# Attention scores on quarters of TensorE: 64 queries by 192 keys a product

## The chip, the cores and the metric

One core of a Trainium2 chip runs the whole program, in one launch. The metric is the device time of that launch in microseconds (us), from runs of the same kernel; a profile of one execution goes with them. TensorE multiplies and has two streams in the profile, PE for products and PEld for the loads of their stationary operands. VectorE is DVE, ScalarE is ACT, GpSimd is POOL, SyncE is SP; "PEq", "SPq" and so on are an engine's sequencer.

## The reference

Attention with a sliding window, then a mixture of eight experts, all in float32. Batch 8, 8 heads, 576 positions, 64 numbers a head:

```python
scores = scale * np.matmul(q, k.transpose(0, 1, 3, 2))
rel = pos[:, None] - pos[None, :]
bias = slopes[:, None, None] * (-np.abs(rel))[None]
mask = (rel >= 0) & (rel < 128)
scores = np.where(mask, scores + bias[None], -1e9)
...
attn = exp(scores - max) / sum
x = attn @ v
```

The rows of x (4608 tokens of 512 numbers) go to two of eight experts each, chosen by the two largest noisy logits: relu(x @ w1[e]) @ w2[e], weighted by the softmax of the two logits. A query sees itself and the 127 keys ahead of it, so a block of 64 queries needs 191 keys.

## The kernel before, in words

**Pairs and groups.** The 64 (batch, head) sets are 32 pairs of heads. A pair's queries and keys lie in one tile `qk`, transposed: head 0 on partitions 0 to 63, head 1 on 64 to 127, first the queries (`QW` columns), then the 576 keys. A pair has five blocks of queries, four of 128 and one of 64, in `GROUPS`: blocks 0 and 1, blocks 2 and 3, and the last block, which is taken for two pairs at once. That makes 32 + 32 + 16 = 80 units.

**A unit** (`unit`, line 612) passes from engine to engine. TensorE computes the scores into two banks of PSUM, one a head (`scores`, line 491; `scores_of_last`, line 510). A block of 128 queries is multiplied with the 128 keys of the block before and its own 128 (block 0 with its own alone), so a product is 64 x 128 queries by 128 or 256 keys, and the products of the two heads stand on the two halves of TensorE's rows. For the last blocks, 64 queries of head 0 and 64 of head 1 stand behind each other in columns 512 to 639 of `qk` with zeros on the other head's partitions, and one product over all 128 rows gives both heads' 192 scores; the next bank takes the next pair.

VectorE folds the two halves into one row of 128 keys (`top`, line 518): a masked copy puts a query's own-block keys over the keys that are out of its window, and a custom instruction (line 516) adds the bias and finds the largest. ScalarE takes the exponentials and their sums (`soft`, line 536). TensorE transposes (line 553), ScalarE or VectorE copies out of PSUM (`evac`, lines 267 and 271), GpSimd splits the two key blocks again (lines 573 and 574), TensorE multiplies with the values (`weigh`, line 576; `weigh_last`, line 591).

**After a batch** the rows are normalised and written to memory (`rows`, `row_major`), the gate's logits are made (`gate`, line 759) and the tokens are routed (`route`). The first expert's first 1024 tokens are begun while attention still runs (`first`, products on lines 1272 and 1316); all the other blocks of tokens follow in a second wave, after the last of attention's memory has been given back.

**The order** is made by a planner while the program is built (`Order`, line 97). Each step is given to its engine with a cost and a rank (`pe(us, rank, ...)`), and an engine takes the step of lowest rank that is ready, by the planner's clock. A step that ScalarE or VectorE may do (`either`) goes to whichever takes it first. TensorE's steps have a mode; `like` (line 185) prefers, among steps of nearly the same rank, one of the mode in use, and a change of mode costs `SWITCH`. The scores of full blocks have the mode "rows", the last blocks "full", as the transposes. There are two pairs of banks for scores (`sb`), five tiles `qk` and five of probabilities (`pr`).

**The start.** GpSimd makes number patterns, VectorE the masks from them (`masks`, line 344), and ScalarE or VectorE copies the bias of each head with its slope (`bias_of`, line 360).

Of the kernel before, what the change touches and what calls it, by code (L numbers as in the profile page):

```python
# [22 lines left out]
NP = H // 2  # L23
QW = 512 + 128
GROUPS = ((0, 1), (2, 3), (4,))
# [202 lines left out]
def attention_moe(ctx: ExitStack, tc: tile.TileContext, qk_, v, w_gate, w_noise, noise, w1, w2,  # L228
# [115 lines left out]
    def masks():  # L344
        def window(out_, rel_):

            nc.vector.tensor_scalar(out_, rel_, 0.0, float(W), op0=OP.is_lt, op1=OP.mult)
            nc.vector.tensor_add(out_, out_, rel_)

        def full():  # L350
            nc.vector.tensor_scalar(own_key, rel, 0.0, None, op0=OP.is_ge)
            window(rel2[:, 0], rel)
            nc.vector.tensor_scalar(rel2[:, 1], rel, 0.0, 2.0 ** 40, op0=OP.is_lt, op1=OP.mult)
            nc.vector.tensor_add(rel2[:, 1], rel2[:, 1], rel)

        def halves():
            nc.vector.tensor_scalar(own_key4, rel4[:, 0:64], 0.0, None, op0=OP.is_ge)
            window(relc4, rel4)

        def bias_of(e, h):  # L360
            copy(e, bias[:, :, h], rel2, scale=slope(h))
            part = slice(h % 2 * 64, h % 2 * 64 + 64)
            copy(e, bias4[part, h // 2], relc4[part], scale=slope(h))

        yield dve(0.14, -40, lambda: nc.vector.tensor_scalar(ident, rel, 0.0, None, op0=OP.is_equal))
        yield dve(0.14, -40, lambda: nc.vector.tensor_scalar(before, rel, 0.0, None, op0=OP.is_lt))
        yield dve(1.0, -40, full)
        yield dve(0.6, -40, halves)
        for g in range(NP):
            for h in (2 * g, 2 * g + 1):  # L370
                yield either(0.56, 0.37, -20 + 5 * g, LATE[9], lambda e, h=h: bias_of(e, h))
            mark(biased[g])
# [118 lines left out]
    def scores(k, blocks, s):  # L491
        qk = qks[k]
        for z, i in enumerate(blocks):
            k0, c = (i - 1) * 128 if i else 0, width(i)
            o = place_of(blocks, z)
            for h in range(2):
                half = slice(h * D, h * D + D)
                nc.tensor.matmul(s[h][:, o:o + c], qk[half, i * 128:i * 128 + 128], qk[half, QW + k0:QW + k0 + c],  # L498
                                 start=True, stop=True)

# [9 lines left out]
    def scores_of_last(k, s):  # L510
        for z in range(2):
            qk = qks[k + z]
            nc.tensor.matmul(s[z][:, 0:192], qk[:, 512:QW], qk[:, QW + S - 192:QW + S], start=True, stop=True)

# [15 lines left out]
    def top_of_last(k, s, p, nm):  # L530
        for z in range(2):
            nc.vector.copy_predicated(s[z][:, 0:64], own_key4.bitcast(U32), s[z][:, W:W + 64])
        for z in range(2):
            biased_and_largest(p[:, z, 0], s[z][:, 0:W], bias4[:, (k + z) % NP], nm[:, z, 0:1])

# [7 lines left out]
    def soft_of_last(g, p, nm, den):  # L543
        for z in range(2):
            pv = p[:, z, 0]
            nc.scalar.activation(pv, pv, AF.Exp, bias=nm[:, z, 0:1], scale=-1.0,
                                 accum_out=den[:, 0, 2 * g + 2 * z:2 * g + 2 * z + 1])

# [6 lines left out]
    def evac(e, blocks, t, pt):  # L555

        if blocks == (4,):
            copy(e, pt[:, :, 0], t[:, 0:2 * W].rearrange("p (z c) -> p z c", z=2))
        else:
            copy(e, pt[:, :, 0:2] if blocks[0] == 0 else pt[:, :, 0:4:2], t.rearrange("p (h z c) -> p h z c", h=2, z=2))  # L560

    def split(blocks, pt):

        if blocks == (4,):
            a, b = (pt[:, :, x].rearrange("p z (h c) -> p z h c", h=2) for x in (0, 1))
            pattern = [[0, 2], [0, 2], [1, 64]]
# [24 lines left out]
    def weigh_last(k, pt, o):  # L591

        t = values_[k // 2]
        for z in range(2):
            for at, kb in ((0, 3), (1, 4)):
                for h in range(2):
                    half, hh = slice(h * D, h * D + D), (2 * z + h) * D
                    nc.tensor.matmul(o[half, z * D:z * D + D], t[:, kb, hh:hh + D], pt[:, z, at, half], start=at == 0, stop=at == 1)

# [12 lines left out]
    def unit(u):  # L612
# [5 lines left out]
        if last:  # L618
# [6 lines left out]
        mark(seated)  # L625
        yield pe((0.77, 0.98, 0.53)[gr], r0, lambda: scores_of_last(k, s) if last else scores(k, blocks, s),
                 mode="full" if last else "rows")
        for z in range(k, k + 1 + last):
# [65 lines left out]
    def rows(b, last, t):  # L694
# [6 lines left out]
        def sums():  # L701
            if last:
                nc.vector.tensor_scalar(den[0:64, 0, 1:H:2], den[64:128, 0, 0:H:2], 1e-9, None, op0=OP.add)
                nc.vector.tensor_scalar(den[0:64, 0, 0:H:2], den[0:64, 0, 0:H:2], 1e-9, None, op0=OP.add)
            else:
# [867 lines left out]
    ranks = ranks1 + [1000 + s for s in range(8 * len(second))]  # L1573

    nc.gpsimd.memset(ones, 1.0)
    nc.gpsimd.memset(one, 1.0)
# [4 lines left out]
    nothing = nc.gpsimd.to_reg(0.0)  # L1581
    order.busy["POOL"], order.busy["DVE"], order.busy["ACT"] = 2.5, 1.5, 1.9
    order.at(2.5, lambda: order.dispatch("POOL"))
    order.at(1.5, lambda: order.dispatch("DVE"))
    order.at(1.9, lambda: order.dispatch("ACT"))
# [100 lines left out]
```

## Time and profile before

| | |
|---|---|
| three runs | 1040.87, 1041.65, 1038.19 us; median 1040.87 |
| span of the profiled execution, first to last instruction | 1039.9 us |
| TensorE busy in it | 1006.7 us (97%), 6952 products |
| VectorE busy | 684.7 us (66%) |
| ScalarE busy | 440.4 us (42%) |
| GpSimd busy | 367.3 us (35%) |
| mean granted clock of TensorE | 0.990 |

For the profiled execution the span is the time that the profile gives; the time of that launch as the runs count it is not listed apart. The page of the profile has each engine's busy time; the views behind it show the same execution by stretches of time, by line, by wait and instruction by instruction. A product's record ends when its last result is out, so records overlap and a busy TensorE need not be working at its peak.

### The profile page before, as it was taken

The page shows a single profiled execution, that of the slowest core. Times are in us where ns is not written, and L with a number is a line of the kernel's source. Part 1 is how long each engine was busy: PE and PEld are TensorE (multiplying, and loading weights), DVE is VectorE, ACT ScalarE, POOL GpSimd, SP SyncE. Part 2 cuts the span into 40 slices and gives each one's busy share as a digit, 9 for nine tenths or more (in the row PEclk, how much of TensorE's full clock was granted, in tenths as well). Part 3 has the DMA queues.
Part 4 walks back from the last instruction along what each step waited for, and adds up shares of the span by engine and source line. Part 5 has one row for each costly group of instructions (what it writes and reads, how often), then busy time and mean ns, then how long its engine had stood idle before and what let it go on. Part 6 is the DMA issues. An engine that isn't in the chain of part 4 may idle for free. (4 is left out here: it accounts for less than half of the span.)

```text
span 1039.9 us, 20426 instructions
## 1 busy us (share of the span) xinstructions
PE 1006.7 (97%) x6952; PEld 613.2 (59%) x6952; DVE 684.7 (66%) x2410; ACT 440.4 (42%) x1218; POOL 367.3 (35%) x572
## 2 busy tenths in 40 slices
PE   8998999989999999999999999999999999999996
PEld 6776766656557645654574457456644754584454
DVE  8988999997756857744777566467636834773311
ACT  8976887762222524332342344134313421442211
POOL 4356686664633203331232233143203320332202
PEclk9999999989999999999999999999999999999998
DMA  9856989835399879893997489859957794864223
GB/s 345 297 173 209 310 306 307 291 72 142 59 251 188 203 200 177 134 207 107 182 205 173 73 175 187 203 78 171 208 156 106 152 189 153 172 132 68 37 24 49
DMA packets 193338, 178.61 MB, mean 172 GB/s; under 512 B 104080, under 2 KB 147376, under 8 KB 193232
## 3 DMA queue, kind: packets, MB, share of 16 engines
q1 hardware_dynamic: 175888, 138.35, 49.2%
q0 software_dynamic: 17344, 38.94, 23.9%
q8 instruction: 55, 0.90, 0.4%
q14 instruction: 51, 0.42, 0.1%
HBM read 117.29 MB, written 40.71 MB: 152 GB/s over the span
## 5 line engine op out<-in xcount | busy, mean ns | idle before, releaser
L1405 POOL DMA_INDIRECT out_dram<-yo,ix x69 | 110.4, 1600 | 497.5 <-ACT yo L267 448.3
L1292 ACT ACTIVATE hh<-bank 128x384 f16<-128x384 f32 (+9 forms) x192 | 92.9, 484 | 449.4 <-PE bank L1272 442.5
L1307 DVE SCALAR_TENSOR_TENSOR hl<-bank,hh 128x384 f16<-128x384 f32 (+9 forms) x200 | 108.8, 545 | 255.9 <-ACT hh L1292 255.0
L1316 PEld LDWEIGHTS <-hh 128*128 128x128 f16 (+1 forms) x944 | 92.2, 98 | 100.2
L1272 PE MATMUL bank<-xh,w1hb 128*128 128x512 f16 (+8 forms) x384 | 127.0, 331 | 0.4 <-DMA xh<-th 0.4
L1272 PE MATMUL bank<-xh,w1lb 128*128 128x512 f16 (+8 forms) x384 | 127.1, 331 | 0.0
L1272 PE MATMUL bank<-xl,w1hb 128*128 128x512 f16 (+8 forms) x384 | 126.9, 330 | 0.1
L1272 PEld LDWEIGHTS <-w1ha 128*128 128x128 f16 x832 | 80.5, 98 | 48.8
L1272 PEld LDWEIGHTS <-w1hb 128*128 128x128 f16 x768 | 75.3, 98 | 55.5 <-issue 2.3
L1272 PE MATMUL bank<-xh,w1ha 128*128 128x384 f16 (+8 forms) x320 | 102.0, 319 | 0.0
L1272 PE MATMUL bank<-xh,w1la 128*128 128x384 f16 (+8 forms) x320 | 102.0, 319 | 0.0
L1272 PE MATMUL bank<-xl,w1ha 128*128 128x384 f16 (+8 forms) x320 | 102.0, 319 | 0.0
L540 ACT ACTIVATE p<-p,nm 128x128 f32<-128x128 f32 x256 | 99.0, 392 | 5.6 <-DVE nm L516 5.6
L1316 PE MATMUL bank<-w2ha,hl 128*128 128x512 f16 x244 | 92.5, 379 | 0.3 <-DVE hl L1307 0.3
L1316 PE MATMUL bank<-w2ha,hh 128*128 128x512 f16 x244 | 92.5, 379 | 0.0
L1316 PE MATMUL bank<-w2la,hh 128*128 128x512 f16 x244 | 92.5, 379 | 0.0
L1316 PE MATMUL bank<-w2hb,hl 128*128 128x512 f16 x228 | 86.4, 379 | 0.7 <-DVE hl L1307 0.7
L1316 PE MATMUL bank<-w2hb,hh 128*128 128x512 f16 x228 | 86.4, 379 | 0.0
L1316 PE MATMUL bank<-w2lb,hh 128*128 128x512 f16 x228 | 86.4, 379 | 0.0
L1219 POOL DMA_INDIRECT xg<-xs_dram,ix x69 | 73.8, 1070 | 32.4 <-issue 14.8
L1316 PEld LDWEIGHTS <-hl 128*128 128x128 f16 x472 | 46.4, 98 | 57.5 <-DVE hl L1307 2.4
L498 PE MATMUL bank<-qk 64*128 64x256 f32 (+1 forms) x512 | 67.1, 385 | 7.0 <-DMA qk<-in_qk_dram 4.6
(250 smaller groups left out, 2036.3 us busy)
## 6 DMA issues: line engine op xcount, KB each, us to landing
raw<-in_w_dram SPq DMA_DIRECT2D x144, 256.0 KB, 4.8
mraw<-in_w_dram SPq DMA_DIRECT2D x56, 512.0 KB, 4.1
qk<-in_qk_dram SPq DMA_DIRECT2D x32, 608.0 KB, 5.3
vraw<-in_v_dram SPq DMA_DIRECT2D x16, 640.0 KB, 6.6
out_dram<-xg SPq DMA_DIRECT2D x10, 1024.0 KB, 7.6
xs_dram<-x SPq DMA_DIRECT2D x32, 256.0 KB, 5.4
xg<-xs_dram,ix POOLq DMA_INDIRECT x69, 5.8
xh<-th SPq DMA_TRANSPOSE x69, 6.0
```

Of the source, the lines that this page charges most:

```text
L498: nc.tensor.matmul(s[h][:, o:o + c], qk[half, i * 128:i * 128 + 128], qk[half, QW + k0:QW + k0 + c], start=True, stop=True)
L540: nc.scalar.activation(pv, pv, AF.Exp, bias=nm[:, z, h:h + 1], scale=-1.0, accum_out=den[:, i, 2 * g + h:2 * g + h + 1])
L1219: yield pool(1.04, rank, lambda: nc.gpsimd.indirect_dma_start(out=xg[0:r], out_offset=None, in_=xs[0:blk.rows], in_offset=bass.IndirectOff ...
L1272: nc.tensor.matmul(t[:, 0:blk.n], wp[:, c], x[:, c, 0:blk.n], start=c == 0 and z == 0, stop=c == 3 and z == 2)
L1292: nc.scalar.activation(o, i, AF.Relu)
L1307: yield dve(0.07 + c * 0.00104, rank - MIDDLE, lambda: nc.vector.scalar_tensor_tensor(hl[:, 0:c], t[:, 0:c], 0.0, hh[:, 0:c], op0=OP.max, ...
L1316: nc.tensor.matmul(blk.y[j][0:r], h[:, cs], wp, start=f == 0 and m == 0, stop=f == 7 and m == 2)
L1405: ins = nc.gpsimd.indirect_dma_start(out=out, out_offset=bass.IndirectOffsetOnAxis(ap=blk.ix[0:r, j:j + 1], axis=0), in_=t[0:r], in_offset ...
```

## The change

Every product of scores becomes one of 64 queries by 192 keys (128 for block 0) on a quarter of TensorE: the head chooses the half of the rows, the half block of queries the half of the columns. Of the 256 scores of a query, the 64 that lie outside its window anyway are no longer computed. The last blocks of two pairs become four such products, and a bank of PSUM now holds one head of both pairs, where it held both heads of one pair; the bias tile, the sums and the product with the values follow. The queries are loaded without the columns of zeros. A quarter of each bank is no longer written by the products; four fills at the start set the banks to zero. The planner's costs and modes are changed for these steps, and its VectorE begins at 2.5 us in place of 1.5.

```diff
-QW = 512 + 128
+QW = S
...
-            part = slice(h % 2 * 64, h % 2 * 64 + 64)
-            copy(e, bias4[part, h // 2], relc4[part], scale=slope(h))
+            part = slice(h // 2 % 2 * 64, h // 2 % 2 * 64 + 64)
+            copy(e, bias4[part, h // 4 * 2 + h % 2], relc4[part], scale=slope(h))
...
-            for h in range(2):
-                half = slice(h * D, h * D + D)
-                nc.tensor.matmul(s[h][:, o:o + c], qk[half, i * 128:i * 128 + 128], qk[half, QW + k0:QW + k0 + c],
-                                 start=True, stop=True)
+            for a in (0, 64):
+                first_, c_ = (a, c - 64) if i else (0, c)
+                for h in range(2):
+                    half = slice(h * D, h * D + D)
+                    nc.tensor.matmul(s[h][a:a + 64, o + first_:o + first_ + c_], qk[half, i * 128 + a:i * 128 + a + 64],
+                                     qk[half, QW + k0 + first_:QW + k0 + first_ + c_], start=True, stop=True)
...
-            nc.tensor.matmul(s[z][:, 0:192], qk[:, 512:QW], qk[:, QW + S - 192:QW + S], start=True, stop=True)
+            for h in range(2):
+                half = slice(h * D, h * D + D)
+                nc.tensor.matmul(s[h][z * 64:z * 64 + 64, 0:192], qk[half, 512:QW], qk[half, QW + S - 192:QW + S],
+                                 start=True, stop=True)
...
-                    nc.tensor.matmul(o[half, z * D:z * D + D], t[:, kb, hh:hh + D], pt[:, z, at, half], start=at == 0, stop=at == 1)
+                    nc.tensor.matmul(o[half, z * D:z * D + D], t[:, kb, hh:hh + D], pt[:, h, at, z * D:z * D + D], start=at == 0, stop=at == 1)
...
-        yield pe((0.77, 0.98, 0.53)[gr], r0, lambda: scores_of_last(k, s) if last else scores(k, blocks, s),
-                 mode="full" if last else "rows")
+        yield pe((0.66, 0.77, 0.43)[gr], r0, lambda: scores_of_last(k, s) if last else scores(k, blocks, s),
+                 mode="quads")
...
-                nc.vector.tensor_scalar(den[0:64, 0, 1:H:2], den[64:128, 0, 0:H:2], 1e-9, None, op0=OP.add)
-                nc.vector.tensor_scalar(den[0:64, 0, 0:H:2], den[0:64, 0, 0:H:2], 1e-9, None, op0=OP.add)
+                lower, upper = (den[z:z + 64, 0].rearrange("p (a b) -> p a b", b=4) for z in (0, 64))
+                nc.vector.tensor_scalar(lower[:, :, 2:4], upper[:, :, 0:2], 1e-9, None, op0=OP.add)
+                nc.vector.tensor_scalar(lower[:, :, 0:2], lower[:, :, 0:2], 1e-9, None, op0=OP.add)
...
+    for t in bank[0:4]:
+        nc.vector.memset(t, 0.0)
...
-    order.busy["POOL"], order.busy["DVE"], order.busy["ACT"] = 2.5, 1.5, 1.9
+    order.busy["POOL"], order.busy["DVE"], order.busy["ACT"] = 2.5, 2.5, 1.9
...
-    order.at(1.5, lambda: order.dispatch("DVE"))
+    order.at(2.5, lambda: order.dispatch("DVE"))
...
-    qk[..., 0:512], qk[..., QW:] = q[..., 0:512], k
-    for h in range(2):
-        qk[:, h, :, 512 + 64 * h:512 + 64 * h + 64] = q[:, h, :, 512:]
+    qk[..., 0:QW], qk[..., QW:] = q, k
```

What is left out here does the same exchange of pair and head in the largest values, the exponentials, the copy and the split of the last blocks (`top_of_last`, `soft_of_last`, `evac`, `split`), with the same number of instructions.

## Rows read from the trace of the kernel before

**Rows 1.** The page, busy time of each engine.
```profile
PE 1006.7 (97%) x6952; PEld 613.2 (59%) x6952; DVE 684.7 (66%) x2410; ACT 440.4 (42%) x1218; POOL 367.3 (35%) x572
```
**Rows 2.** Windows by stage: from:to, length, busy (records), clock, DMA share, GB/s.
```profile
13.00:100.00 87.00, 84.19 (x872) 61.19 (x873) 79.21 (x439) 71.35 (x307) 46.61 (x101) 1.00 0.74 249
20.00:60.00 40.00, 40.00 (x414) 30.11 (x414) 38.35 (x207) 38.05 (x169) 15.81 (x33) 1.00 0.86 291
100.00:220.00 120.00, 109.31 (x1151) 79.83 (x1151) 115.26 (x591) 93.64 (x368) 82.47 (x164) 0.97 0.87 283
220.00:262.00 42.00, 42.00 (x362) 27.77 (x359) 35.54 (x145) 18.43 (x62) 22.09 (x42) 0.96 0.39 100
328.00:1039.90 711.90, 697.25 (x4105) 400.20 (x4103) 402.42 (x1037) 227.53 (x405) 185.39 (x205) 0.99 0.72 145
```
**Rows 3.** Timeline of TensorE, 213 to 233: start, length, records, [idle before, releaser].
```profile
213.06 0.55 PE L875 MATMUL bank<-hot,hot 128*80 128x64 f16 x10 [3.01 <-DVE gw L1235]
...
231.14 0.33 PE L1272 MATMUL bank<-xhe,w1ha 128*128 128x384 f16 x1
```
**Rows 4.** Waits (total, times, longest): VectorE 13:100, then 100:220, then TensorE.
```profile
DVE xu L271 <- PE bank L589: 2.2, 2, 1.4
DVE lt L775 <- PE bank L770: 1.6, 2, 1.0
...
DVE x L737 <- PE bank L734: 1.1, 2, 0.8
DVE bank L524 <- PE bank L498: 0.6, 2, 0.4
...
PE bank L498 <- DMA qk<-in_qk_dram: 4.6, 1, 4.6
```
**Rows 5.** Timeline of TensorE, 59.6 to 70.6, runs of records of one line.
```profile
61.17 0.69 PE L598 MATMUL bank<-pT,vraw 128*64 128x64 f32 x16
...
62.81 1.13 PE L498 MATMUL bank<-qk 64*128 64x256 f32 x8
63.87 0.66 PE L553 MATMUL bank<-ident,p 128*128 128x128 f32 x4
64.46 1.06 PE L759 MATMUL bank<-xu,wgn 128*32 128x512 f32 x8
...
66.13 0.82 PE L513 MATMUL bank<-qk 128*128 128x192 f32 x4
...
69.57 0.93 PE L498 MATMUL bank<-qk 64*128 64x128 f32 x8
```
**Rows 6.** Records of lines 498 (69.5:70.4) and 598 (61.1:61.7): ns min/median/max, starts.
```profile
L498 PE MATMUL bank<-qk x8: 272/374/378, 69.6 to 70.1; 64*128 64x128 f32 x4, 64*128 64x256 f32 x4
...
L598 PEld LDWEIGHTS bank<-pT,vraw x16: 132/138/138, 61.2 to 61.6; 128*64 128x64 f32 x16
```
**Rows 7.** Timeline of all engines, 0 to 16.
```profile
1.45 0.24 DVE L365 TENSOR_SCALAR ident<-raw 128x128 f32<-128x128 f32 x1 [1.45 <-POOL raw L1577]
...
3.62 4.10 ACT L267 ACTIVATE bias<-raw 64x128 f32<-64x128 f32 x13 [0.15 <-DVE raw L348]
...
3.98 0.52 POOL L413 MEMSET xg<- 128x512 f32 x1
...
6.24 0.50 DVE L524 COPY_PREDICATED bank<-own_key,bank 128x128 f32<-128x128 uint32 x2 [2.65 <-PE bank L498]
...
11.05 0.69 DVE L271 COPY pT<-bank 128x512 f32<-128x512 f32 x1
```
**Rows 8.** Windows of line 498 alone: PE and PEld busy (records), clock, DMA.
```profile
13.00:100.00 87.00, 28.16 (x224) 18.14 (x224) 1.00 0.74 249
100.00:220.00 120.00, 29.32 (x235) 18.84 (x237) 0.97 0.87 283
```
**Rows 9.** Lines of VectorE, 13 to 100: busy us, mean ns, idle before.
```profile
L1177 DVE TENSOR_REDUCE wam<-raw 128x1 f32<-128x512 f32 x8 | 5.4, 672 | 0.0
```
**Rows 10.** A window behind a long wait of TensorE, columns as in rows 2.
```profile
213.40:216.90 3.50, 3.39 (x25) 2.15 (x23) 3.36 (x12) 0.78 (x2) 2.91 (x6) 0.51 1.09 258
```

More of the change, by code (lines that the diff above doesn't have):

```diff
@@ L530, in top_of_last @@
     def top_of_last(k, s, p, nm):
[L531 to L534, printed above, removed]
+        for h in range(2):
+            nc.vector.copy_predicated(s[h][:, 0:64], own_key4.bitcast(U32), s[h][:, W:W + 64])
+        for h in range(2):
+            biased_and_largest(p[:, h, 0], s[h][:, 0:W], bias4[:, k % NP + h], nm[:, h, 0:1])
     def soft(g, blocks, p, nm, den):
@@ L543, in soft_of_last @@
     def soft_of_last(g, p, nm, den):
[L544 to L547, printed above, removed]
+        for h in range(2):
+            pv = p[:, h, 0]
+            nc.scalar.activation(pv, pv, AF.Exp, bias=nm[:, h, 0:1], scale=-1.0,
+                                 accum_out=den[:, 0, 2 * g + h:2 * g + h + 1])
     def trans(p, t, nh):
@@ L557, in evac @@
         if blocks == (4,):
-            copy(e, pt[:, :, 0], t[:, 0:2 * W].rearrange("p (z c) -> p z c", z=2))
+            copy(e, pt[:, :, 0], t[:, 0:2 * W].rearrange("p (h c) -> p h c", h=2))
         else:
@@ L564, in split @@
         if blocks == (4,):
-            a, b = (pt[:, :, x].rearrange("p z (h c) -> p z h c", h=2) for x in (0, 1))
+            a, b = (pt[:, :, x].rearrange("p h (z c) -> p h z c", z=2) for x in (0, 1))
             pattern = [[0, 2], [0, 2], [1, 64]]
```

## The prediction

> **What bounds the kernel now.** I read the page first. TensorE is busy 97% of the span, no other engine over 66% [rows 1]. So I cut the span into stages [rows 2]. From 328 us on, the second wave of expert products holds TensorE for 697 of 712 us; the change touches nothing there. Scores (lines 498 and 513) lie ahead of that, before 262 us. From 13 to 100 us TensorE is busy 84.2 of 87 us and waits only 2.8 in all; VectorE has 79.2, ScalarE 71.4. From 100 to 220 it is VectorE that is full, 115.3 of 120, and TensorE lacks 10.7. From 220 to 262 TensorE is full again, because at 231 the first expert products arrive and fill every hole [rows 3]. The view of waits says the same from the other side [rows 4]: in the first stretch VectorE waits for TensorE (2.2 + 1.6 = 3.8 us lead its list), and in the second TensorE waits for VectorE (3.0 us at once before 213 [rows 3]), while VectorE's own waits for TensorE have shrunk to 1.1 + 0.6 = 1.7.
>
> Past 220 us the end is the sum of TensorE's remaining work: whatever has been done earlier by then comes off the end. So the question is how much of the saved TensorE time turns into earlier work, and how much into waiting.
>
> **What one unit of scores costs.** Three units are shown, from the first record's start to the last one's end [rows 5]: 0.93 us for blocks 0 and 1, 1.13 for blocks 2 and 3, 0.82 for the last blocks. Each float32 product is two records (32 pairs make 64 such units of eight records, 512). A record of 128 columns lasts 272 ns, one of 256 lasts 378: 0.83 ns a column, or 53 ns for 64 columns [rows 6]. The products of two heads lie side by side: blocks 2 and 3 make four steps of 256 columns, 4 x 0.213 = 0.85; blocks 0 and 1 two steps of 128 and two of 256, 0.64. Both leave 0.28 or 0.29 us. The last unit, in the shape of the transposes ahead of it, is four steps of 192 columns one after another, 4 x 0.16 = 0.64, and leaves 0.18, the tail of a last record. So going into a shape costs about 0.1; going out the same, since the line behind the second unit starts 1.06 after it began (62.81 to 63.87), 0.21 over its steps.
>
> **What the change takes off.** (1) Blocks 1 to 3 stream 192 columns instead of 256 in each step, if four quarters run side by side. Four steps in a unit of blocks 2 and 3 save 4 x 0.053 = 0.213; 32 units, 6.8 us. In blocks 0 and 1 only block 1 gets shorter: 0.107 x 32 = 3.4. Block 0 still streams 128.
> (2) A last unit becomes two steps instead of four: 0.32 x 16 = 5.1 us. It leaves the transposes' shape for its own, so it may pay up to two more changes, or none beside another unit of scores: 0 to 3.2 us. I take one each, 1.6, since the planner prefers like beside like; 3.5 stays.
> That is 13.7 us of TensorE time. Four abreast with quarters in both directions is not in this trace. The nearest rows: the gate's products, four strips of 32 output rows, are eight records of 512 columns in 1.06 us; at 0.43 for a step, one after another would be 3.4, so four do run abreast. And line 598 sends sixteen records of 64 columns, weights as narrow as the new ones, in 0.69 us with the last one's tail, a pair in some 0.06 [rows 5]: short loads keep up. The records double (512 to 1024, 64 to 128), which these rows say costs nothing. Bounds of (1) and (2): from 13.7 saved to none, and the rivals below go beyond.
>
> Those loads of line 598 start while products of the same 128 rows are in flight: sixteen loads of 138 ns, their starts within some 0.4 us [rows 6]. By these rows the saving is 13.7 us. A rule speaks against it: the Trainium skill (TensorE: Matmul & The Clock Gate, Part 3: Packing small matmuls — row/col tiling) says that a weight load overlaps running products only where the row group differs, and two of the four quarters of a step share theirs. By that rule it would be about nothing, the third rival; the trace does not bear the rule out for column strips.
>
> (3) The four fills on VectorE at the start, 128x512 in PSUM. Nearest rows: GpSimd's fill of that size 0.52 us, VectorE's copy of that size 0.69, so 2.1 to 2.8 us in all [rows 7]. VectorE's first work is at 1.45, when the first number pattern is there, and it idles 2.65 us before its first score work at 6.24. Fills begun by 0.8 end between 2.9 and 3.6 and push the masks back by 1.5 to 2.1, which that idle time hides. On ScalarE it does not hide: its bias copies, 3.62 to 7.72, wait for the masks (0.15 us before them), and its exponentials come behind them. Bounds 0 and 2.1 us, less what the planner hands to VectorE; I take 1.4. Against it stands what the first scores save, below. If the cover were gone (VectorE busy up to 6.24) the whole 2.1 would show.
> (4) The loads of queries and keys shrink by a twentieth (1216 to 1152 columns). TensorE waits on them only at the start, 4.6 us [rows 4], and 1/19 of that is at most 0.3. I take none: elsewhere they are hidden behind four loads in reserve.
> (5) VectorE's and ScalarE's work on the last blocks, now by head instead of by pair, has the same number and size of instructions, the sums of line 703 too: 0, even uncovered. The exchange of pairs and heads in the transposed copy and line 598 is addressing: 0.
> (6) The planner gets other costs and a new shape, so the order moves on every queue. No row prices that. What one ill-placed step can cost now is the 3.0 us that TensorE waits at its longest [rows 3]. Bounds -3 and +3; I take 0.
>
> **What of it reaches the end.** Of the 512 records of line 498, 224 lie between 13 and 100 us and 235 between 100 and 220 [rows 8]; I spread the last units alike. The first stretch then saves 13.7 x 224/512 = 6.0 us. VectorE must follow, and what it waits for TensorE there now is 3.8, so 3.8 counts. The second saves 6.3, of which by the same reason 1.7 counts; 4.6 becomes new waiting. The other 53 records are 1.4 us, half of it after 220, where it counts, half in the start: 0.7 - 1.4 = -0.7. Sum 3.8 + 1.7 + 0.7 - 0.7 = 5.5 us. The span shown is 1039.9, and the median of the runs 1040.9, 1.0 more, with runs from 1038.2 to 1041.7; against the median that makes 1035.4. Less than 0.3% (3.1 us) could not be told from no change.
>
> **The rivals.** First, VectorE takes it all: it is full already from 20 to 60 us (38.4 of 40) and from 100 to 220 [rows 2], so a faster TensorE only waits. For it: the busy shares. Against it: part of that can slide to where VectorE is freer, as the eight reductions of weights (5.4 us, line 1177) before 100 [rows 9]. It leaves the 0.7 after 220 less the start: 1040 to 1041, no change. The Trainium skill (TensorEngine Tiling (Array Packing), PSUM Bottleneck) has this as its warning, that tiling speeds up products and not the emptying of PSUM; this trace agrees from 100 to 220 and not before.
> Second, the clock. It falls to its lower level, 1.2 GHz, at times: granted 0.51 from 213.4 to 216.9, just after TensorE had waited 3.0 us for VectorE [rows 3, 10], and the stages' means of 0.97 and 0.96 [rows 2] put it at an estimated 7.2 and 3.4 us in all. A stretch like that one loses up to 1.7 us of TensorE. With 4.6 us more of waiting there could be more of them; four, 6.8 us, would eat the gain: 1041.
> Third, weights not hidden: each step of quarters shows its 64-column load, 0.06. Four steps give 0.24: blocks 2 and 3 lose their 0.213, blocks 0 and 1 grow by 0.13 (4.2 us in all), last units keep 0.2 of 0.32 (3.2, less 1.6 of changes). Net +3.5 of TensorE, about two thirds of it felt: 1043.
> Fourth, slower: the change does not do what it says, and the quarters of one head run one after the other, two abreast in place of four. Its place is every unit. Blocks 2 and 3: eight steps of 0.16 against 0.85, +0.43; blocks 0 and 1 likewise +0.43; the last units stay. 64 x 0.43 = 27 us more, all of the 44% before 100 felt, of the 46% after it little more than the 10.7 of waiting does not hold: 12 + 2 + 1, with 1.6 of changes and the start some 18: 1059. It decides once a step of four takes over 0.21.
>
> **How the numbers follow.** The forecast has 0.64 (1027 to 1038: all 13.7 saved, or half of my sum). VectorE's rival 0.16, the clock 0.07, weights 0.06, two abreast 0.07. Faster is 0.63 of the first, 0.03 of the second and 0.02 of the clock: 0.68. Slower is two abreast, 0.07, half of the weights, 0.03, and 0.02 each of the clock and of the second, where a worse order comes on top: 0.14. The rest, 0.18, is the same. The range, 1027 to 1043, leaves out mostly the fourth and the ends.
>
> **What would show it.** Right: four records of 192 columns starting within some 20 ns, a step each 0.16 us; units of 0.82 and 0.92 us, and 0.5 to 0.6 for the last; TensorE's waits from 100 to 220 grown by 4 to 5 us, VectorE's idle time from 13 to 100 (7.8) down by about 4; the first expert product some 5 us before 231. Wrong: steps of 0.21 or more; a first exponential more than 1.4 us later; more stretches at 0.5 of the clock; a first expert product no earlier than 231 with less attention left behind it would move the gain to another place, and with as much behind it would end it.

## The result, and the profile after

The changed kernel takes 1046.89 us (median of 7 runs, 1042.83 to 1050.25) against 1040.41 (7 runs, 1037.52 to 1041.88) for the kernel before on the same chip: a ratio of 1.0055, 95% interval 1.003 to 1.0081. By the medians it is 6.5 us slower; the forecast was 5.5 us faster, 1035.4, with 1043 as the upper end of its range. The span of the profiled execution is 1045.1 us, 5.2 more than before.

The page of the changed kernel, busy time by engine [rows 1]: 576 products more, TensorE's busy time 6.6 us less, VectorE's and GpSimd's 2.9 and 4.0 more.

```profile
PE 1000.1 (96%) x7528; PEld 597.5 (57%) x7528; DVE 687.6 (66%) x2410; ACT 440.6 (42%) x1222; POOL 371.3 (36%) x572
```

The products of scores do what was forecast. The timeline of TensorE in the changed kernel, 59 to 72 us (start, length, records) [rows 5]:

```profile
59.99 0.78 PE L500 MATMUL bank<-qk 64*64 64x128 f32 x16
...
61.28 0.88 PE L500 MATMUL bank<-qk 64*64 64x192 f32 x16
62.10 1.07 PE L765 MATMUL bank<-xu,wgn 128*32 128x512 f32 x8
...
66.54 0.56 PE L517 MATMUL bank<-qk 64*64 64x192 f32 x8
```

A unit of blocks 2 and 3 lasts 0.88 us (1.13 before), one of blocks 0 and 1 0.78 (0.93), a last one 0.56 (0.82). Windows of the scores' lines alone, 0 to 262 us (from:to, length, PE busy, PEld busy, clock, DMA share, GB/s), give the sum. The kernel before, lines 498 and 513:

```profile
0.00:262.00 262.00, 67.09 (x512) 43.38 (x512) 0.98 0.75 244
...
0.00:262.00 262.00, 13.56 (x64) 10.01 (x64) 0.98 0.75 244
```

and the changed kernel, lines 500 and 517:

```profile
0.00:262.00 262.00, 57.29 (x1024) 35.27 (x1024) 0.99 0.74 241
...
0.00:262.00 262.00, 9.62 (x128) 3.99 (x128) 0.99 0.74 241
```

80.65 us became 66.91: 13.7 us saved on these lines, the sum of terms (1) and (2). Not all of it is TensorE's gain: the 288 records of transposes in the same window take 48.1 us where they took 45.2. Windows of line 553 in the kernel before and of line 558 in the changed one:

```profile
0.00:262.00 262.00, 45.22 (x288) 31.82 (x288) 0.98 0.75 244
```
```profile
0.00:262.00 262.00, 48.11 (x288) 31.63 (x288) 0.99 0.74 241
```

**Where it went.** I cut the span at two marks that mean the same work in every version: the first product of the first wave of experts (it reads `xhe`) and the first of the second wave (it reads `xh`). Windows of the kernel before (columns as in [rows 2]):

```profile
0.00:231.10 231.10, 212.81 (x2165) 154.83 (x2166) 213.55 (x1136) 184.95 (x753) 140.76 (x303) 0.98 0.79 260
...
231.10:328.60 97.50, 97.20 (x688) 58.50 (x687) 68.93 (x240) 28.32 (x61) 41.11 (x64) 1.00 0.72 155
```

Windows of the changed kernel, the last two rows being the stretches whose idle time the prediction gave numbers for:

```profile
0.00:223.30 223.30, 201.59 (x2737) 139.13 (x2737) 210.03 (x1125) 182.23 (x745) 141.11 (x301) 0.98 0.79 262
...
223.30:333.50 110.20, 100.76 (x689) 58.40 (x686) 75.75 (x252) 31.19 (x74) 43.61 (x67) 0.97 0.64 145
333.50:1045.10 711.60, 697.71 (x4108) 400.02 (x4106) 401.86 (x1034) 227.17 (x404) 186.55 (x205) 1.00 0.71 145
...
13.00:100.00 87.00, 86.42 (x1220) 60.49 (x1212) 82.05 (x461) 81.95 (x354) 52.72 (x115) 1.00 0.76 257
...
100.00:220.00 120.00, 103.74 (x1397) 72.06 (x1393) 114.30 (x586) 87.73 (x344) 82.55 (x157) 0.97 0.83 268
```

Up to the first mark the changed kernel is 7.8 us ahead. The second wave takes 711.6 us, as before (711.3). All of the loss is between: 110.2 us for 97.5, with the same number of products (689 and 688), so no attention was left behind. Of these 12.7 us, 9.1 are waiting (110.20 - 100.76 = 9.44, against 0.30), and 3.6 are products that ran longer, at a mean granted clock of 0.97 for 1.00 (an estimated 0.03 x 110.2 = 3.3). In the sum: -7.8 + 12.7 + 0.3 = 5.2.

The waits of the changed kernel in that stretch, 262 to 345 us (total, times, longest; columns as in [rows 4]):

```profile
PE bank L1322 <- DVE hl L1313: 6.8, 2, 4.6
...
DVE fit L1246 <- DMA xg<-xs_dram,ix: 5.9, 2, 4.5
```

The same two rows in the kernel before:

```profile
DVE fit L1240 <- DMA xg<-xs_dram,ix: 3.3, 3, 2.3
...
PE bank L1316 <- DVE hl L1307: 0.3, 1, 0.3
```

The longer of TensorE's two waits, 4.6 us, is half of all its waiting there. The timelines of GpSimd, VectorE and TensorE in the changed kernel show how it comes about:

```profile
303.17 0.96 POOL L1225 DMA_INDIRECT xg<-xs_dram,ix  x1 [13.69 <-DVE ix L1023]
304.44 0.95 POOL L1225 DMA_INDIRECT xg<-xs_dram,ix  x1 [0.30 <-issue]
305.69 0.95 POOL L1225 DMA_INDIRECT xg<-xs_dram,ix  x1 [0.30 <-issue]
...
306.94 1.61 POOL L1411 DMA_INDIRECT out_dram<-yo,ids  x1 [0.22 <-issue]
...
308.85 1.56 POOL L1411 DMA_INDIRECT out_dram<-yo,ids  x1 [0.27 <-issue]
...
310.72 1.55 POOL L1411 DMA_INDIRECT out_dram<-yo,ids  x1 [0.26 <-issue]
312.58 1.50 POOL L1225 DMA_INDIRECT xg<-xs_dram,ix  x1 [0.30 <-issue]
...
324.09 0.69 DVE L1246 TENSOR_REDUCE fit<-xg 128x1 f32<-128x512 f32 x1 [4.53 <-DMA xg<-xs_dram,ix]
...
326.48 0.75 DVE L1313 SCALAR_TENSOR_TENSOR hl<-bank,hh 128x256 f16<-128x256 f32 x2
...
326.95 0.61 PE L1322 MATMUL bank<-w2ha,hl 128*128 128x512 f16 x1 [4.64 <-DVE hl L1313]
```

The fourth gather of a block of tokens for the second wave stands on GpSimd behind three scatters of results of the first wave. VectorE comes to the step that needs it (line 1246) and stands there 4.53 us, until 324.09, 11.5 us after the gather was issued; the halves `hl` that TensorE needs for the first wave's second products are queued behind that step and come at 326.48. TensorE waits 4.64 us, and after that it runs at the lower level (1.2 GHz) for a while, as a window of the same kernel shows:

```profile
326.90:329.90 3.00, 2.95 (x8) 1.04 (x9) 2.25 (x12) 0.72 (x1) 0.00 (x0) 0.51 0.52 104
```

In the kernel before GpSimd issues the four gathers in a row, before the first of the scatters (308.67):

```profile
298.63 1.23 POOL L1219 DMA_INDIRECT xg<-xs_dram,ix  x1 [8.61 <-DVE ix L1017]
300.17 0.94 POOL L1219 DMA_INDIRECT xg<-xs_dram,ix  x1 [0.31 <-issue]
301.42 0.95 POOL L1219 DMA_INDIRECT xg<-xs_dram,ix  x1 [0.30 <-issue]
302.67 0.95 POOL L1219 DMA_INDIRECT xg<-xs_dram,ix  x1 [0.30 <-issue]
```

The other long wait, 2.2 us (2.17, at 284.56), stands in the same way behind a gather of the first wave (`xg<-xs_dram,cl`), for which VectorE waits 3.3 us.

So the theory after the profile: the products gain what was forecast, and the order that the planner makes from its new numbers loses more than that where the two waves meet.

### The profile page after: what moved, and what is told of

The parts are those of the page before. It is cut to its first block, busy times and chain, and to the rows that moved or that the text cites. A ratio compares the mean times of both kernels' runs of the same rounds, so it can differ in the third digit from the quotient of the medians.

```text
span 1045.1 us, 21578 instructions
## 1 busy us (share of the span) xinstructions
PE 1000.1 (96%) x7528; PEld 597.5 (57%) x7528; DVE 687.6 (66%) x2410; ACT 440.6 (42%) x1222; POOL 371.3 (36%) x572
## 5 line engine op out<-in xcount | busy, mean ns | idle before, releaser
L1298 ACT ACTIVATE hh<-bank 128x384 f16<-128x384 f32 (+9 forms) x188 | 90.8, 483 | 434.5 <-PE bank L1278 413.5
L1322 PEld LDWEIGHTS <-hh 128*128 128x128 f16 (+1 forms) x944 | 92.2, 98 | 100.1 <-issue 1.4
L1225 POOL DMA_INDIRECT xg<-xs_dram,ix x69 | 75.9, 1100 | 39.8 <-DVE ix L1023 19.5
L1322 PEld LDWEIGHTS <-hl 128*128 128x128 f16 x472 | 46.5, 99 | 66.0 <-DVE hl L1313 10.7
L267 ACT ACTIVATE th<-xg,fit 128x512 f16<-128x512 f32 (+5 forms) x76 | 54.3, 718 | 49.6 <-DVE fit L1238 38.3
```

The source lines that it names most:

```text
L267: nc.scalar.activation(o, i, AF.Copy, **kw)
L1225: yield pool(1.04, rank, lambda: nc.gpsimd.indirect_dma_start(out=xg[0:r], out_offset=None, in_=xs[0:blk.rows], in_offset=bass.IndirectOff ...
L1298: nc.scalar.activation(o, i, AF.Relu)
L1322: nc.tensor.matmul(blk.y[j][0:r], h[:, cs], wp, start=f == 0 and m == 0, stop=f == 7 and m == 2)
```

## The experiments

Each ratio is to the kernel before on the same chip. "Profiled" is the time of the one execution that the profile shows; the last three columns are its stages: to the first mark, between the marks, the second wave.

| run | median us | ratio [95%] | profiled us | to first | between | second |
|---|---|---|---|---|---|---|
| before | 1040.41 | 1 | not listed | 231.1 | 97.5 | 711.3 |
| after | 1046.89 | 1.0055 [1.003, 1.0081] | 1046.89 | 223.3 | 110.2 | 711.6 |
| e1_old_order | 1038.48 | 0.9974 [0.9958, 0.999] | 1037.14 | 226.2 | 98.2 | 711.0 |
| e2_new_order | 1052.35 | 1.0097 [1.0064, 1.0131] | 1052.08 | 230.7 | 103.8 | 715.8 |
| e3_new_costs_only | 1043.38 | 1.002 [1.0003, 1.0038] | 1043.08 | 223.9 | 105.2 | 712.3 |
| e4_new_mode_only | 1040.81 | 0.9992 [0.9974, 1.0009] | 1039.8 | 225.9 | 100.1 | 712.1 |
| e5_no_fills | 1034.35 | 0.9931 [0.9909, 0.9953] | 1034.13 | 226.1 | 96.9 | 709.4 |
| e6_vector_load | 1038.62 | 0.9971 [0.9952, 0.999] | 1035.39 | 227.3 | 97.0 | 709.4 |
| e7_gather_later | 1048.73 | 1.0063 [1.0039, 1.0087] | 1050.45 | 223.0 | 101.0 | 724.7 |
| e8_nudged | 1045.5 | 1.0049 [1.0027, 1.0071] | 1050.66 | 232.7 | 99.0 | 717.2 |
| e9_junction | 1043.29 | 1.0002 [0.9984, 1.002] | 1043.19 | 224.4 | 103.7 | 713.3 |
| e10_no_fills_new_order | 1047.4 | 1.0028 [1.0008, 1.0049] | 1051.18 | 224.4 | 113.3 | 711.8 |
| e11_fills_only | 1043.08 | 1.0002 [0.9992, 1.0013] | 1043.1 | 231.7 | 98.4 | 711.2 |
| e12_junction_no_fills | 1041.74 | 1.0 [0.9984, 1.0017] | 1043.63 | 226.4 | 102.3 | 713.2 |
| e13_old_order_again | 1037.28 | 0.9977 [0.9957, 0.9997] | 1034.04 | 226.2 | 97.0 | 709.1 |
| e14_no_fills_again | 1033.91 | 0.9944 [0.9924, 0.9964] | 1034.53 | 226.0 | 96.9 | 709.9 |
| e15_scalar_load | 1037.09 | 0.9972 [0.9954, 0.999] | 1037.82 | 226.8 | 97.4 | 711.9 |
| e16_gpsimd_load | 1032.9 | 0.9938 [0.9915, 0.9961] | 1032.76 | 224.4 | 96.9 | 709.7 |

How far a single execution can be trusted shows where one kernel was profiled twice. e1 and e13 agree at the first mark (226.2 and 226.2) and part behind it, by 1.2 us between the marks and 1.9 in the second wave; e5 and e14 part by 0.1, nothing and 0.5. So behind the first mark a stage that differs by some 2 us says little. And some profiled executions lie far from their medians: e8's is the slowest of its five runs, 5 us above the median, e10's is 4 us above, e13's 3 us below.

**Products and order apart.** e1 is the changed kernel with the planner's numbers of before, so that every engine's sequence is that of before, apart from the fills (in the traces the two agree instruction by instruction):

```diff
-        yield pe((0.66, 0.77, 0.43)[gr], r0, lambda: scores_of_last(k, s) if last else scores(k, blocks, s),
-                 mode="quads")
+        yield pe((0.77, 0.98, 0.53)[gr], r0, lambda: scores_of_last(k, s) if last else scores(k, blocks, s),
+                 mode="full" if last else "rows")
...
-    order.busy["POOL"], order.busy["DVE"], order.busy["ACT"] = 2.5, 2.5, 1.9
+    order.busy["POOL"], order.busy["DVE"], order.busy["ACT"] = 2.5, 1.5, 1.9
...
-    order.at(2.5, lambda: order.dispatch("DVE"))
+    order.at(1.5, lambda: order.dispatch("DVE"))
```

e2 is the reverse: the products of before, with the planner's numbers of the change; its sequences are those of the changed kernel.

> All of the change's products, fills and loads, but the planner's old costs, modes and start, so every engine works off the same order as before the change. Theory A (the quarters do what they should, the loss is the new order's): faster than before by 4 to 9 us, 1031 to 1037, since the record-level saving of some 13 us is then set against an order that fits the transfers; the wait of 4.6 us behind VectorE near 327 us is gone. Theory B (VectorE and ScalarE bound the attention, and what TensorE saves only comes back as waiting): 1038 to 1042. Theory C (something in the quarters or the fills costs more than the records show): 1043 to 1048, as with the change.

> The products, loads and start of before, but the planner's new costs, mode and start, so the order of the change. Theory A: slower than the change, 1048 to 1060, because the new order's waits stay and TensorE has 10 to 14 us more to do. Theory B: 1043 to 1049, as the change, since TensorE's own work then does not matter. Theory C: 1038 to 1042, as before.

e1 is 2.8 us faster than the kernel before, e2 some 10 us slower (0.0097 x 1041). The order is worth +0.97% with the old products (e2) and about +0.8% with the new (after against e1); the products with their fills -0.26% in the old order (e1) and about -0.4% in the new (after against e2; the comparisons of after with e1 and with e2 are between sets of runs). By its time e1 misses its first theory (1031 to 1037) and lies where the second was put (1038 to 1042: what TensorE saves comes back as waiting). e2, at 1052.4, came in the range of the first theory alone. So the order costs what the change was to gain and more, and in the old order a good part of the saving does come back as waiting. Windows of e1:

```profile
0.00:226.20 226.20, 201.87 (x2742) 140.81 (x2743) 212.49 (x1138) 183.99 (x752) 141.11 (x303) 0.98 0.80 261
...
226.20:324.40 98.20, 97.63 (x689) 58.41 (x687) 68.77 (x241) 28.48 (x64) 41.18 (x65) 1.00 0.76 154
```

In the old order the middle stage has no hole (98.2 us) and the first mark is 4.9 us earlier than in the kernel before. In the new order the old products lose 6.3 us there too, and 4.5 in the second wave. Windows of e2:

```profile
230.70:334.50 103.80, 98.88 (x689) 58.28 (x686) 75.56 (x250) 30.85 (x72) 42.94 (x66) 0.98 0.65 154
334.50:1050.30 715.80, 698.12 (x4108) 400.10 (x4106) 401.37 (x1034) 227.23 (x404) 186.32 (x205) 1.00 0.70 144
```

**Which number moved it.** e3 takes the new costs alone, e4 the new mode alone; e8 is the kernel before with one cost raised by a hundredth:

```diff
-        yield pe((0.77, 0.98, 0.53)[gr], r0, lambda: scores_of_last(k, s) if last else scores(k, blocks, s),
+        yield pe((0.78, 0.98, 0.53)[gr], r0, lambda: scores_of_last(k, s) if last else scores(k, blocks, s),
```

> The change with the planner's new costs, but its old modes and VectorE's old start. Another order again. Theory A: the time depends on how the order happens to meet the transfers, anything from 1032 to 1050, and goes with TensorE's waits between 220 and 345 us, not with the records of the scores, which stay as in the change. Theories B and C: 1043 to 1048, like the change.

> The change with the planner's new mode (all scores alike), but its old costs and VectorE's old start. Theory A: as for the run before, 1032 to 1050 by TensorE's waits between 220 and 345 us. Theories B and C: 1043 to 1048.

> The kernel before, with one cost of the planner changed by a hundredth of a microsecond (0.77 to 0.78 for the scores of blocks 0 and 1) and nothing else. It reorders as many instructions as the change does. Theory A (an order that has not been fitted to the transfers loses several microseconds, whatever made it): 1043 to 1052. Rival (the new costs and the new mode make a worse order of their own): 1039 to 1043.

Neither number alone gives the whole loss: the costs put 7.0 us into the middle stage (105.2 against e1's 98.2), the mode 1.9, which is hardly more than two executions of one kernel differ by. VectorE's later start, the third number, was not tried alone. The time of e3 (1043.4) fits all its theories, that of e4 (1040.8) the first alone. And e8, whose products are those of before, is 0.49% slower by nothing but another order, as its first theory had it; in its profiled execution, the slowest of five, the second wave shows it most (717.2 us for 711.3). So another order can cost as much as the gain that was sought. That the kernel before has an order that suits it better than most I infer from this run and from e2, e3 and e4; one nudge is no survey of orders.

**The place.** e7 and e9 are the changed kernel, with a longer time in the planner for the gathers of the second wave, all of them in e7, those of its first three blocks in e9:

```diff
-        yield max(order.now + 3.4, order.transfer(order.now, 2048.0 * r))
+        yield max(order.now + (8.0 if blk in second[:3] else 3.4), order.transfer(order.now, 2048.0 * r))
```

> The change, with one number of the planner altered: it counts 8 us instead of 3.4 from the issue of a gather of the second wave to its rows, so VectorE's scaling of those rows stands later in its queue. The order of attention stays. Theory A (the loss is VectorE standing in its queue at a gather that has not landed, with the products' halves behind it): TensorE's waits between 262 and 345 us fall from 7 us to under 3, the first product of the second wave comes at 326 to 329 us instead of 333, and the time is 1038 to 1043. Rival (the loss lies elsewhere): 1045 to 1049.

> The change, with the planner's 8 us in place of 3.4 for the gathers of the first three blocks of the second wave alone: attention and the second wave from its fourth block on keep the change's order. (With all blocks altered the second wave began at 324 us and not at 333, but lost 13 us later on, where its order had changed as well.) Theory A (the change loses its time between the first product of the first wave, at 223 us, and that of the second, at 333, where TensorE waits behind VectorE at a gather): the second wave begins at 324 to 329 us and the end follows, 1036 to 1042. Rival (what is gained there is always lost again later): 1044 to 1049.

Both shorten the middle stage, to 101.0 and 103.7 us from 110.2. e7 pays for it behind (724.7 us), and its time is the rival's. e9 keeps most, and with it the change stands level with the kernel before: 1.0002 against 1.0055, with intervals that do not meet; its time, 1043.3, lies between what the theory (1036 to 1042) and the rival (1044 to 1049) gave. So over half a per cent of the loss hangs on the order around the meeting of the waves. Windows of e9:

```profile
224.40:328.10 103.70, 98.43 (x682) 58.18 (x679) 69.56 (x228) 28.80 (x68) 42.58 (x66) 0.97 0.58 146
```

The hole did not close: 5.3 us of waiting are left, and the clock is still at 0.97. But it is another wait. GpSimd still issues the fourth gather behind three scatters (315.65), yet VectorE no longer stands at it, and TensorE's wait of 4.64 us is gone. What is left at its longest stands behind the gather of the first wave, which the edit did not touch. The timelines of VectorE and TensorE in e9:

```profile
284.82 0.69 DVE L1246 TENSOR_REDUCE fit<-xg 128x1 f32<-128x512 f32 x1 [4.45 <-DMA xg<-xs_dram,cl]
...
286.02 0.61 PE L1322 MATMUL bank<-w2ha,hl 128*128 128x512 f16 x1 [3.31 <-DVE hl L1313]
```

That wait was 2.2 us in the changed kernel. No run gave this gather more time too, and none moved the fourth gather ahead of the scatters.

**The fills.** Here the first unit of full blocks in each pair of banks streams all 256 keys, which writes every quarter of the banks once and makes the fills needless (the added scores are masked like the others outside the window): e5 and e14 on e1, e10 on the changed kernel, e12 on e9. e11 is the kernel before with the four fills, and e13 is e1 once more, beside e14 on one chip.

```diff
+            whole = (id(s), blocks[0]) not in written
+            written.add((id(s), blocks[0]))
...
-                first_, c_ = (a, c - 64) if i else (0, c)
+                first_, c_ = (a, c - 64) if i and not whole else (0, c)
...
-    for t in bank[0:4]:
-        nc.vector.memset(t, 0.0)
```

> The run with the old order, without the four fills; the first unit of full blocks in each pair of banks streams all 256 keys instead, so that nothing unwritten is read. Theory A with the fills on the path (the first exponentials come 1.4 us later than before the change, and VectorE and ScalarE are full until 60 us, so the delay goes through): 1.0 to 1.5 us faster than the run with the old order, about 1037.3. Rival (the delay is used up in the holes between 60 and 100 us): no difference, 1038.2 to 1038.8.

> The change and its order, without the four fills; the first unit of full blocks in each pair of banks streams 256 keys. If the fills cost what they did in the old order (4 us): 1042 to 1044. If they are worth only the 1.4 us that the first exponentials come later: 1045 to 1046. If the order decides what becomes of a start that is earlier: anything up to 1048.

> The kernel before with the four fills on VectorE ahead of its masks and nothing else. If the fills delay the first exponentials by 1.4 us and the full engines pass that on: slower than before by 1 to 4 us, ratio 1.001 to 1.004. If TensorE, which binds before 100 us with the old products, makes up for it: within 0.5 us, ratio 0.9995 to 1.0005.

> The run with the later gathers of three blocks, and without the fills. Theory A: the sum of both, 1033 to 1040, near the run with the old order and no fills (1034.4) or better. Rival: 1042 to 1047.

> The change's products in the order of before, fills kept, as in the run of that kernel above, here beside the same kernel without the fills on one chip. If the fills cost something (theory): 0.995 to 0.999 of the kernel before, and 2 to 5 us behind the kernel without them. If they cost nothing (rival): within 1.5 us of it.

> The change's products in the order of before, without fills. If the fills cost something: 0.991 to 0.995 of the kernel before, first expert product near 226 us. If not: the two intervals cover each other, both near 0.995.

In the old order the kernel without fills is the faster one twice: 0.9931 against e1's 0.9974, and on one chip 0.9944 against 0.9977, where the intervals just overlap, by 0.0007. e13 and e14 came where their theory had them; e5, at 1034.4, gained more than its own (1.0 to 1.5 us). The other pairs show 0.0027 (after and e10, overlapping) and 0.0002 (e9 and e12), and fills added to the old products (e11) cost nothing that can be told, as its rival said. e12, expected at 1033 to 1040 as the sum of two gains, came at 1041.7. The profiled executions of e13 and e14 differ by 0.2 us at the first mark and by 0.5 at the end, the other way; but that of e13 is one of its three fastest of twelve. So the price lies between nothing (e11, e12) and 0.43%, some 4.5 us (e5 against e1). In the old order it does not lie before the first mark, where the four executions with and without fills differ by 0.2 us at most; no row shows its place behind it. e10, at 1047.4, fits only the loosest of its forecasts (anything up to 1048): it has the wait of the changed kernel again, longer, with 113.3 us between the marks. TensorE's waits in it, 225 to 345 us:

```profile
PE bank L1326 <- DVE hl L1317: 9.9, 3, 6.2
```

Without fills in the old order the change is faster than the kernel before, by 0.56% (e14) and 0.69% (e5).

**Who sets the pace before the first mark.** Spare work on one engine in each of the 80 units, into a tile that nothing reads: on VectorE in e6 (on e1), on ScalarE in e15 and on GpSimd in e16 (both on e14).

```diff
+        nc.vector.memset(dummy, 0.0)
```
```diff
+        nc.scalar.activation(dummy, ident[:, 0:64], AF.Exp)
```
```diff
+        nc.gpsimd.memset(dummy, 0.0)
```

> The run with the old order, with one more small fill of a spare tile on VectorE in each of the 80 units of scores, some 0.1 us each, 8 to 10 us in all. If VectorE binds attention now and takes up what TensorE saves: slower than the run with the old order by 5 to 9 us, 1043 to 1047. If its full look is work that can slide: by 0 to 3 us, 1038 to 1041.

> The kernel without fills, with one more exponential of 64 columns into a spare tile on ScalarE at the head of each of the 80 units: an estimated 0.3 us each, 64 of them (19 us) ahead of the first expert product. If ScalarE's step of each unit sets TensorE's pace before the first wave (theory): that product 5 us or more later than near 226, the time 5 to 15 us above the run without load. If nothing on ScalarE binds (rival): under 1.5 us later, time within 2 us.

> The kernel without fills, with a fill of a spare tile of 128x64 on GpSimd at the head of each of the 80 units' splits: an estimated 0.1 to 0.3 us each, 6 to 19 us ahead of the first expert product. If GpSimd's split sets TensorE's pace (theory): that product 3 us or more later than near 226, the time 3 to 10 us above the run without load. If not (rival): under 1.5 us later, time within 2 us.

The groups of the spare work, one of e6 (64 of its 80), two of e15, one of e16 (busy us, mean ns, idle before):

```profile
L526 DVE MEMSET dummy<- 128x64 f32 x64 | 7.2, 112 | 0.1
```
```profile
L547 ACT ACTIVATE dummy<-ident 128x64 f32<-128x64 f32 x64 | 16.5, 258 | 0.0
L555 ACT ACTIVATE dummy<-ident 128x64 f32<-128x64 f32 x16 | 4.1, 258 | 0.0
```
```profile
L574 POOL MEMSET dummy<- 128x64 f32 x80 | 13.6, 170 | 0.2
```

These are 9.0 us of records on VectorE, 20.6 on ScalarE and 13.6 on GpSimd. But the records overlap those beside them, and the engines' busy time up to the first mark grew by less: on VectorE by 2.9 us (212.5 in e1, above, to 215.4), on ScalarE by 9.9 (184.1 in e14 to 194.1), on GpSimd by 6.8 (141.3 to 148.1). Windows of e6, then of e14, e15 and e16:

```profile
0.00:227.30 227.30, 201.84 (x2741) 140.07 (x2742) 215.38 (x1218) 184.55 (x752) 141.19 (x303) 0.98 0.80 260
```
```profile
0.00:226.00 226.00, 202.25 (x2741) 141.02 (x2742) 210.61 (x1134) 184.14 (x752) 141.28 (x303) 0.97 0.79 262
```
```profile
0.00:226.80 226.80, 200.32 (x2741) 139.35 (x2742) 211.78 (x1134) 194.06 (x827) 140.33 (x302) 0.98 0.80 261
```
```profile
0.00:224.40 224.40, 200.25 (x2741) 139.41 (x2742) 209.84 (x1134) 184.39 (x752) 148.06 (x380) 0.98 0.80 263
```

The first mark came 1.1 us later with the work on VectorE, 0.8 later with that on ScalarE, and 1.6 earlier with that on GpSimd. So ScalarE's and GpSimd's amount of work does not set TensorE's pace there. Of the 2.9 us on VectorE over a third came through, so e6 is too light a load to say that VectorE does not set the pace.

The times: e6 stands level with e1 (0.9971 and 0.9974), e16 1.0 us below e14, within the intervals. e15 is 3.2 us above e14, more than its rival allowed (2) and less than its theory (5); the two intervals overlap, but on one chip each of e15's twelve runs is slower than each of e14's seven. Only 0.8 us of it lie before the first mark; where the rest comes from was not followed up.

## Why the prediction was wrong

**The step that failed is (6).** It said that the order moves on every queue and then: "No row prices that. What one ill-placed step can cost now is the 3.0 us that TensorE waits at its longest [rows 3]. Bounds -3 and +3; I take 0." Three things in it were wrong. The order is worth some 8 to 10 us here (after against e1, and e2), not 3. And it did not move to better or worse alike: the one other order tried without the change (e8) was 5 us worse, e2 and e3 are each worse than the same products in the old order, and e4 was 2.3 us behind e1 in the median, with overlapping intervals. And I looked for the price only where the change is, before 220 us, while it fell due at 262 to 330, where I had written that "the end is the sum of TensorE's remaining work". That held in the kernel before, with 0.30 us of waiting between the marks; with the gathers and scatters in another sequence TensorE waited 9.44 us there and ran 3.6 us longer. The rows of that stretch were there to be read, and they show how short the margin was: VectorE stood 2.3 us at its longest for a gather. So was the planner's number: it counts at least 3.4 us from a gather's issue to its rows, where the median on the page of the kernel before is 5.8. e9, with later gathers for three blocks, takes back 0.53% of the 0.81% that the order costs the new products; the rest stays open as to its place.

**Right in the main: (1) and (2).** The scores' lines save 13.7 us of their own busy time, with units of 0.88, 0.78 and 0.56 us against 0.92, 0.82 and 0.5 to 0.6. The records start in fours within 20 ns, as the signs said. All products on TensorE before the first mark shrank by less, 212.8 to 201.6 us (11.2): the transposes took 46.4 us there for 44.0. They grew with the new products in both orders (to 262 us, 48.0 in e1 and 48.1 in the changed kernel, 46.5 in e14) and not with the old products in the new order (45.4 in e2). The 1.6 us that term (2) set aside for changes of shape are within the 13.7; the transposes' 2.4 stand outside it, and why they last longer no run shows. The rivals of weights not hidden and of two abreast fall by the units: the first would make a unit of blocks 2 and 3 about 1.16 us (four steps of 0.16 with a load of 0.06 each, and the tail of 0.28), the second longer still. The records of line 500 in such a unit of the changed kernel, 61.25 to 62.1 us (columns as in [rows 6]):

```profile
L500 PEld LDWEIGHTS bank<-qk x16: 129/133/133, 61.3 to 61.7; 64*64 64x64 f32 x16
L500 PE MATMUL bank<-qk x16: 322/323/373, 61.3 to 61.8; 64*64 64x192 f32 x16
```

Sixteen loads begin within 0.4 us, while products of 322 ns on the same rows are in flight. The Trainium skill (TensorE: Matmul & The Clock Gate, Part 3: Packing small matmuls — row/col tiling) lets a weight load overlap only products of another row group; quarters that share a row group kept their pace here, 0.88 us for a unit, so the measurement decides against that rule in this shape.

**Partly right, with its reason open: the split of the saving.** I let 5.5 us reach the end, fills included, and the rest become waiting for VectorE. In the old order the split came out so at the first mark, 4.9 us earlier in e1 of 10.9 us less busy time (212.8 to 201.9), with TensorE's idle time up from 18.3 to 24.3. In the runs 2.8 to 3.1 us reach the end with fills (e1, e13), about half of the forecast, and 6.2 to 6.5 without (e5, e14); the 1.4 us set aside for the fills fits neither e11 nor these pairs. Of the signs, TensorE's waits from 100 to 220 grew by 5.6 us (10.7 to 16.3; I said 4 to 5) and VectorE's idle time from 13 to 100 fell by 2.9, not 4 (7.8 to 4.9). The first rival, VectorE taking it all, falls: the first mark came 4.9 us earlier, and e1 is faster than the kernel before. Whether VectorE takes the half that did not arrive is open, since e6 put only 2.9 us more on it, and 1.1 of them showed. (The Trainium skill, TensorEngine Tiling (Array Packing), PSUM Bottleneck, warns of just that rival; e1 does not bear it out in full.) The waits of TensorE in the changed kernel from 100 to 220 are many and short. The head of the view of waits:

```profile
PE bank L500 <- DVE nm L521: 3.5, 7, 1.2
```

Seven waits make 3.5 of the 16.3 us, none over 1.2. That a unit's time around its chain of engines sets the pace, and not any engine's load, would fit; no run here shortened the chain, so it stays open beside VectorE's load.

**Right: (3) at the start.** Fills took 2.1 us and the first exponential came 1.4 us later, as forecast. The timeline of the changed kernel:

```profile
0.98 2.11 DVE L1582 MEMSET bank<- 128x512 f32 x4 [0.98 <-PEq L1681]
...
9.02 0.40 ACT L545 ACTIVATE p<-p,nm 128x128 f32<-128x128 f32 x1
```

and of the kernel before:

```profile
7.63 0.39 ACT L540 ACTIVATE p<-p,nm 128x128 f32<-128x128 f32 x1
```

At the first mark e13 and e14 differ by 0.2 us, so most of the delay was caught up in the profiled executions. Terms (4) and (5), both taken as 0, were not tested by themselves.

**The clock**, the second rival, came true in part and elsewhere: its estimated 3.3 us lie between the marks, after waits that the order made. From 100 to 220 the granted clock is 0.97 in both kernels.

## What to carry to other kernels

Where a planner makes the order from costs, a change of those costs is a change of its own: build the new instructions in the old order first, and let the order move only afterwards. If such an order may have been chosen among many, reckon with its loss and price it at the junctions of stages, where engines stand in line behind a transfer. A gain on the bounding engine counts only until the next place where the order leaves that engine without a reserve. A load put on an engine as a test is to be measured by the busy time that it adds, not by the sum of its records.

## What was not expected of the hardware

A gather issued behind three scatters on GpSimd was used 11.5 us after its issue, by an engine that had stood waiting for it for 4.53 us, where the median from issue to landing is 5.8 us on the page of the kernel before. After TensorE's wait of 4.64 us the granted clock was 0.51 for some 3 us (326.9 to 329.9), and a product that lasts 0.38 us took 0.63. Work that adds 20.6 us of records on ScalarE, 9.9 of busy time before the first mark, moved that mark by 0.8 us, though ScalarE was busy 184.1 of 226 us there. And two executions of one kernel (e1 and e13) agree to 0.1 us after 226 us of attention and part by 3.1 us behind it; what differs between them was not followed up.
